# Head 0, the centroids and the last tokens' activations turned on TensorE; the means of v in one matmul per query block; a new written-out order

## The chip, the cores and the metric

One core of a Trainium2 chip runs the whole program. The metric is the device time of one execution in microseconds (us). Engine names: PE is TensorE, PEld its weight loads, DVE is VectorE, ACT is ScalarE, POOL is GpSimd, SP is SyncE, which issues most DMAs.

## The reference, cut to what matters

Three stages follow each other: attention restricted to clusters, a feed-forward layer, and a soft mixture of experts.

```python
# q, k, v: (2, 8, 768, 64); centroids: (8, 16, 64); 16 pairs of batch and head in all
q_assign = argmax(q_n @ c_n.T); k_assign = argmax(k_n @ c_n.T)
scores = where(q_assign[:, None] == k_assign[None], q @ k.T / 8, -1e9)
attn = exp(scores - max(scores)); attn /= sum(attn) + 1e-9
x = attn @ v                                   # as (1536, 512)
h = x @ w_in                                   # (512, 2048)
x = (h * clip(h + 3, 0, 6) / 6) @ w_out        # (2048, 512)
logits = x @ phi                               # 32 slots, 4 for each of 8 experts
slots = softmax(logits, over tokens).T @ x
out = softmax(logits, over slots) @ experts(slots)   # relu(s @ w1[e]) @ w2[e]
```

A query whose cluster holds no key sees only masked scores, so the softmax is even and its output is the mean of v over all keys. The kernel adds that mean separately.

## The kernel before, in words

Work is cut into *heads* i = 0 to 15 (a batch and a head, 768 queries and keys, six tiles of 128) and *tokens* t = 0 to 11 (tiles of 128 rows of x). Numbers are held as a high and a low float16 part, so that a product of two float32 numbers is made of float16 matmuls: `high` (ACT) rounds to float16, `low` (POOL) subtracts it from the float32 number.

For each head, `cast_hi` and `cast_lo` split q and k into the tile `qk1`. A DMA transpose (L356) turns its twelve 128x128 blocks into `qk1t`. `as_mm` (L385) multiplies that with the turned, normalised centroids `ct` (L793, also a DMA transpose), `as_max` finds the cluster of each row as a one-hot tile `oh` with five short DVE operations (L390 to L404), `as_put` (L411, L412) writes it next to q and k in the tile `qk2`, and a second DMA transpose (L415) gives `qk2t`. `maxq` and `maxr` (L452 on PE, L468 on DVE) take the largest masked score of each query, `shift` (L475, L477) writes it into `qk2t`, `scores` (L490, L494), `exps` (L531, L538) and `pv` (L564 to L585) make the attention output, and `finish` divides. `cnt_mm` counts the keys of each cluster and makes the mean of v for empty clusters (`mv`, a high and a low part side by side), and the last call of `pv` for a head adds it with two matmuls for each of six query blocks (L584, L585).

The input weights of the feed-forward layer are read as 64-bit numbers and narrowed to 32 bits: `narrow` is one ACT operation (L809) and three on DVE (L811, L814, L819) for each chunk of 128x1024. Chunks are called `wi` and `wod`. `wphi1` to `wphi3` fold phi into w_out.

For each token, `xtrans` turns x, `hid` (L633) multiplies with w_in, twelve matmuls of 512 columns for each of four column blocks. `act` makes the activation in halves of two column blocks: ACT (L650), DVE (L652), `high` on ACT, `low` on POOL (L322), giving `ghl`. Then each half is turned into `gt`: for tokens 0 to 5 both halves by a DMA transpose (L661); for tokens 6 to 10 the first half by a DMA transpose and the second by sixteen PE transposes into PSUM (L669) which ACT (L675) and DVE (L673) copy out; for token 11 all on PE. `logits` (L684, L685) needs both halves, then `colmax` (its transpose is L712), `dweights`, `dispatch` (L755) and `cweights`.

The end multiplies the slots with the experts' weights, 36 chunks of 1 MB called `wk`, loaded by SP. The first 15 chunks fit into buffers that are free once attention has ended; the next four take the place of w_in (`wq`), so the last of them waits for the last `hid`; the following ones wait for buffers of the last tokens' activations, and the rest for earlier chunks to be used.

The order of all this on every engine is written out by hand: each step is a generator, and `ORDER` is a list of generator numbers, each entry advancing one of them to its next `yield`. Every engine works through its own instructions in that order. `ROOMS` fixes which buffer each tile gets; PSUM has three large rooms (of `pss`) and two small ones (`psm`). SP and ACT issue DMAs in that same order, so a transfer that must wait holds back all behind it in its queue.

Of the kernel before, what the change touches and what calls it, by code (L numbers as in the profile page):

```python
# [1367 lines left out]
```

## Time and profile before

| what | value |
|---|---|
| median of three runs | 501.41 us (500.82 to 502.27) |
| the profiled execution | 496.43 us, its span 494.6 us |
| busy: PE, PEld | 439.8 us (89%), 276.1 us (56%) |
| busy: DVE, ACT, POOL | 305.0 us (62%), 310.9 us (63%), 258.1 us (52%) |
| chain that ended last, by engine | PE 61%, DVE 19%, ACT 5%, issue 4%, DMA 4%, POOL 3%, SP's queue 2% |
| moved by DMA | 96.89 MB, mean 196 GB/s |

The span runs from the first to the last instruction. The busy time of an engine is the time in which one of its instructions is on record; matmuls overlap, so a busy PE is not PE at its peak. The shares are means over stages with different limits.

### The profile page before, as it was taken

What the parts mean: (1) busy time and instruction counts of PE and PEld (TensorE: products, weight loads), DVE (VectorE), ACT (ScalarE), POOL (GpSimd) and SP (SyncE); (2) the same over time, 40 slices, a digit from 0 to 9 for tenths busy, and PEclk for the clock granted to TensorE, in tenths of its full rate; (3) what the DMA queues carried; (4) which work ended last, traced back from release to release, by engine and by line L of the source; (5) the groups of instructions that cost most, each with busy time, mean ns of one, the idle gap of its engine ahead of it and who ended that gap; (6) DMA issues with size and microseconds to landing.
All of it is one profiled execution on the core that took longest, in us unless ns stands there. A gap on an engine that the chain in (4) does not pass through costs nothing.

```text
span 494.6 us, 11908 instructions
## 1 busy us (share of the span) xinstructions
PE 439.8 (89%) x4920; PEld 276.1 (56%) x4920; DVE 305.0 (62%) x514; ACT 310.9 (63%) x551; POOL 258.1 (52%) x232
## 2 busy tenths in 40 slices
PE   0379999999999799999999999999999999678884
PEld 0236778767778565756656556664455545442343
DVE  2788988999978999859785556324243333521213
ACT  5587776798777788888857767754245445511112
POOL 4545356456966878788757858763333323400000
PEclk9999999999999999999999999999999999989998
DMA  8985963945956999917308444346998886699998
GB/s 210 257 217 129 235 176 81 194 95 156 248 125 175 245 246 196 261 40 148 88 17 166 130 118 89 126 121 107 287 329 184 252 256 177 226 371 380 378 321 278
DMA packets 139447, 96.89 MB, mean 196 GB/s; under 512 B 102016, under 2 KB 125056, under 8 KB 139392
## 3 DMA queue, kind: packets, MB, share of 16 engines
q1 hardware_dynamic: 134272, 90.29, 69.0%
q10 hardware_dynamic: 5120, 5.83, 3.5%
q8 instruction: 38, 0.62, 0.5%
q14 instruction: 17, 0.14, 0.1%
HBM read 64.06 MB, written 7.34 MB: 144 GB/s over the span
## 4 chain that ended last, share of the span: by engine, by line
PE 61%; DVE 19%; ACT 5%; issue 4%; DMA 4%; POOL 3%; SPq 2%; DVEq 0%; ACTq 0%; POOLq 0%
PE h L633 21%; DVE m L468 6%; PE st L490 5%; PE st L494 5%; PE acc L564 4%; PE sm L452 4%; PE e L1237 3%; PE acc L577 2%; PE acc L569 2%; PE acc L570 2%; POOL ghl L322 2%; SPq L947 1%; PE o L1274 1%; DVE r L652 1%; DMA qf<-in_q_dram 1%
## 5 line engine op out<-in xcount | busy, mean ns | idle before, releaser
L322 POOL TENSOR_TENSOR pp<-p,pp 128x768 f16<-128x768 f32 x64 | 115.3, 1807 | 43.1 <-ACT pp L315 30.6
L633 PE MATMUL h<-wq,xt 128*128 128x512 f16 x576 | 133.9, 379 | 0.0
L468 DVE TENSOR_REDUCE m<-sm 128x1 f32<-128x768 f32 x96 | 89.5, 952 | 21.7 <-PE sm L452 20.9
L633 PEld LDWEIGHTS <-xt 128*128 128x128 f16 x576 | 53.4, 98 | 60.7 <-issue 4.2
L322 POOL TENSOR_TENSOR ghl<-r,ghl 128x1024 f16<-128x1024 f32 (+1 forms) x25 | 50.3, 2011 | 65.4 <-ACT ghl L315 60.1
L538 ACT ACTIVATE p<-st 128x768 f32<-128x768 f32 x64 | 51.5, 805 | 26.3 <-PE st L494 20.1
L315 ACT ACTIVATE pp<-p 128x768 f16<-128x768 f32 x64 | 53.8, 841 | 5.0 <-PE acc L577 3.8
L652 DVE SCALAR_TENSOR_TENSOR r<-r,h 128x1024 f32<-128x1024 f32 (+1 forms) x26 | 29.6, 1138 | 36.1 <-ACT r L650 36.0
L452 PE MATMUL sm<-qk2t 80*128 80x384 f16 x192 | 48.3, 343 | 3.5 <-DVE m L468 3.2
L490 PE MATMUL st<-qk1t 128*128 128x384 f16 x192 | 48.6, 336 | 2.3 <-DVE m L468 1.9
L494 PE MATMUL st<-qk2t 102*128 102x384 f16 x192 | 48.6, 335 | 0.7 <-DVE qk2t L477 0.7
L564 PEld LDWEIGHTS acc<-v,pp 128*128 128x128 f32 x384 | 46.0, 192 | 2.9 <-PE st L494 0.7
L564 PE MATMUL acc<-v,pp 128*128 128x65 f32 x384 | 47.1, 274 | 0.3 <-DVE xa L597 0.3
L650 ACT ACTIVATE r<-h,b_relu 128x1024 f32<-128x1024 f32 (+1 forms) x26 | 27.2, 1046 | 15.6 <-PE h L633 9.4
L322 POOL TENSOR_TENSOR qk<-qf,qk 128x384 f16<-128x384 f32 x16 | 15.4, 962 | 39.5 <-ACT qk L315 36.9
L315 ACT ACTIVATE ghl<-r 128x1024 f16<-128x1024 f32 (+1 forms) x26 | 25.6, 988 | 15.4 <-DVE r L652 11.1
L569 PE MATMUL acc<-v,pp 128*128 128x65 f16 x384 | 32.2, 192 | 0.9 <-DVE mv L437 0.9
L531 ACT ACTIVATE pp<-st 128x768 f32<-128x768 f32 x32 | 25.4, 803 | 11.4 <-PE st L494 11.3
L570 PE MATMUL acc<-v,pp 128*128 128x64 f16 x384 | 32.2, 194 | 0.0
L385 PE MATMUL as<-ct,qk1t 128*128 128x16 f16 x384 | 12.1, 170 | 21.0 <-DMA ct<-cin 12.8
L569 PEld LDWEIGHTS <-pp 128*128 128x128 f16 x384 | 27.7, 99 | 5.3 <-issue 1.9
L570 PEld LDWEIGHTS <-pp 128*128 128x128 f16 x384 | 26.0, 96 | 4.1 <-issue 1.1
(185 smaller groups left out, 804.0 us busy)
## 6 DMA issues: line engine op xcount, KB each, us to landing
wk<-in_moe_w_dram SPq DMA_DIRECT2D x60, 512.0 KB, 7.2
wi<-in_moe_w_in_dram SPq DMA_DIRECT2D x16, 512.0 KB, 5.3
wod<-in_moe_w_out_dram SPq DMA_DIRECT2D x16, 512.0 KB, 5.7
wos<-wo ACTq DMA_DIRECT2D x8, 512.0 KB, 4.4
wk<-wos SPq DMA_DIRECT2D x8, 512.0 KB, 4.4
qf<-in_q_dram SPq DMA_DIRECT2D x16, 192.0 KB, 3.0
kf<-in_k_dram SPq DMA_DIRECT2D x16, 192.0 KB, 3.2
vf<-in_v_dram SPq DMA_DIRECT2D x16, 192.0 KB, 3.0
```

What stands on the lines that cost most here:

```text
L315: nc.scalar.activation(out, in_, AF.Copy, scale=scale)
L322: (nc.vector if e == "v" else nc.gpsimd).tensor_tensor(out=out, in0=in_, in1=hi, op=ALU.subtract)
L452: nc.tensor.matmul(s[:, j, 0:384], d["qk2t"][0:80, n], d["qk2t"][0:80, NT + 3 * j : NT + 3 * j + 3], start=True, stop=True,)
L468: nc.vector.tensor_reduce(out=d["m"][:, n : n + 1], in_=s[:, :, 0:384], op=ALU.max, axis=AX.XY)
L490: nc.tensor.matmul(s[:, j, 0:384], d["qk1t"][:, NT + t], d["qk1t"][:, 3 * j : 3 * j + 3], start=True, stop=False)
L494: nc.tensor.matmul(s[:, j, 0:384], d["qk2t"][0 : 96 + NT, NT + t], d["qk2t"][0 : 96 + NT, 3 * j : 3 * j + 3], start=False, stop=True,)
L538: nc.scalar.activation(p32, s[:, :, 0:384], AF.Exp, scale=sc_exp)
L564: nc.tensor.matmul(o, p32[:, j, r * P : (r + 1) * P], d["v32"][:, t], start=(t == 0 and n == 0), stop=False)
L569: nc.tensor.matmul(o, hi, v1[:, t, 0:65], start=(t == 0 and n == 0), stop=False)
L570: nc.tensor.matmul(o[:, 0:64], hi, v1[:, t, 65:129], start=False, stop=False)
L633: nc.tensor.matmul(s[:, fb % 2], xt[:, lhs], wq[fb][:, hl, kk], start=(n == 0), stop=(n == 11))
L652: nc.vector.scalar_tensor_tensor(out=g, in0=r, scalar=6.0 * SG, in1=sf, op0=ALU.min, op1=ALU.mult)
```

## The change

It has six parts.

1. Head 0's `qk1` and `qk2` are turned by twelve PE transposes each, into a large PSUM room, copied out by ACT (first half) and DVE (second half), instead of two DMA transposes. Heads 1 to 15 keep theirs.
2. The centroids are turned by two PE transposes and a DVE copy.
3. The first halves of tokens 8, 9 and 10 are turned on PE like their second halves.
4. `mv` holds its high part on partitions 64 to 79 and its low part on 80 to 95. `as_put` writes the one-hot twice (32 columns), so one matmul for each query block adds both.
5. In `wphi3`, two DVE operations become one on ACT and one on POOL.
6. `ORDER` and `ROOMS` are new throughout.

```diff
+    def turned(i, nm, out, t):
+        if i:
+            nc.sync.dma_start_transpose(out=out, in_=t.rearrange("p a n d -> p (a n d)"))
+            return
+        tp = pss(f"t0_{nm}").bitcast(F16)
+        for a in range(2):
+            for n in range(NT):
+                nc.tensor.transpose(tp[:, a, n * P : (n + 1) * P], t[:, a, n], ident16)
+        yield
+        for a, fn in ((0, nc.scalar.copy), (1, nc.vector.tensor_copy)):
+            fn(out[:, a * NT : (a + 1) * NT], tp[:, a, 0 : NT * P].rearrange("p (n q) -> p n q", q=P))
...
-        nc.sync.dma_start_transpose(out=d["qk1t"], in_=t.rearrange("p a n d -> p (a n d)"))
+        yield from turned(i, "qk1", d["qk1t"], t)
...
-        nc.sync.dma_start_transpose(out=d["qk2t"], in_=z.rearrange("p a n d -> p (a n d)"))
+        yield from turned(i, "qk2", d["qk2t"], z)
...
-                nc.tensor.matmul(o, e, mv[64:96, 0:65], start=False, stop=False)
-                nc.tensor.matmul(o[:, 0:64], e, mv[64:96, 65:129], start=False, stop=(n == NT - 1))
+                nc.tensor.matmul(o, e, mv[64:96], start=False, stop=(n == NT - 1))
...
-        if t < NT or (f0 == 0 and t < NTOK - 1):
+        if t < NT or (f0 == 0 and t < NTOK - 4):
             nc.sync.dma_start_transpose(
...
-        nc.sync.dma_start_transpose(out=ct, in_=cin.rearrange("p a d -> p (a d)"))
+        tp = psm("ctt").bitcast(F16)
+        for a in range(2):
+            nc.tensor.transpose(tp[:, a * P : (a + 1) * P], cin[:, 2 * a : 2 * a + 2].rearrange("p a d -> p (a d)"), ident16)
+        yield
+        nc.vector.tensor_copy(ct, tp[:, 0 : 2 * P].rearrange("p (a q) -> p a q", q=P))
...
-        nc.vector.tensor_copy(wp2[:, 4 * j : 4 * j + 4, 0:NS], wf)
-        nc.vector.tensor_tensor(
-            out=wp2[:, 4 * j : 4 * j + 4, NS : 2 * NS], in0=wf, in1=wp2[:, 4 * j : 4 * j + 4, 0:NS], op=ALU.subtract
-        )
+        high("a", wp2[:, 4 * j : 4 * j + 4, 0:NS], wf)
+        yield
+        low("p", wp2[:, 4 * j : 4 * j + 4, NS : 2 * NS], wf, wp2[:, 4 * j : 4 * j + 4, 0:NS])
...
 ORDER = (
-    "3 0 3 0 6 1 6 3 6 6 787 4 7 54 4 7 7 3 101 2 8 7 54 788 54 788 789 55 8 101 54 793 55 11 150 11 12 9 2 9 790 10 "
+    "3 3 0 2 6 0 6 6 1 7 11 11 12 4 4 6 7 7 2 787 3 7 54 7 3 54 788 3 101 54 54 788 8 103 793 55 101 789 790 8 55 "
```

What the new order does is seen in the engines' instructions. First, DVE at the start of the program, before the change; `nw` is the narrowing of a chunk of w_in, `as`, `mx` and `oh` are head 0's cluster assignment.

```order
L791 COPY cin_139<-cin_139 128x64
L811 TENSOR_SCALAR nw_i0_0_219<-nw_i0_0_219 128x1024
L814 SCALAR_TENSOR_TENSOR nw_i0_0_219<-wi_0_0_146,nw_i0_0_219 128x1024
L390 TENSOR_REDUCE mx_0_225<-as_0_191 128x12
L391 TENSOR_TENSOR as_0_191<-as_0_191,mx_0_225 128x192
L399 TENSOR_TENSOR as_0_191<-as_0_191,rank_87 128x192
L402 TENSOR_REDUCE mx2_0_252<-as_0_191 128x12
L404 TENSOR_TENSOR oh_0_254<-as_0_191,mx2_0_252 128x192
L819 SCALAR_TENSOR_TENSOR wi_0_0_146<-wi_0_0_146,nw_i0_0_219 128x1024
```

The same place after the change:

```order
L814 COPY cin_209<-cin_209 128x64
L350 COPY qk1t_0_172<-t0_qk1_173 128x768
L820 COPY ct_92<-ctt_220 128x256
L838 TENSOR_SCALAR nw_i0_0_224<-nw_i0_0_224 128x1024
L841 SCALAR_TENSOR_TENSOR nw_i0_0_224<-wi_0_0_198,nw_i0_0_224 128x1024
L846 SCALAR_TENSOR_TENSOR wi_0_0_198<-wi_0_0_198,nw_i0_0_224 128x1024
L406 TENSOR_REDUCE mx_0_267<-as_0_232 128x12
L407 TENSOR_TENSOR as_0_232<-as_0_232,mx_0_267 128x192
L415 TENSOR_TENSOR as_0_232<-as_0_232,rank_88 128x192
L418 TENSOR_REDUCE mx2_0_278<-as_0_232 128x12
L420 TENSOR_TENSOR oh_0_280<-as_0_232,mx2_0_278 128x192
```

Two copies out of PSUM have come in, and all three narrowing operations of the first chunk now stand ahead of head 0's assignment, where only two did.

Second, ACT after the change, where `as_put` of head 0 (L428, L434) stands behind the first step of the second chunk's narrowing (L836 of `nw_i0_1`); before, that chunk's step came after `as_put`.

```order
L836 ACTIVATE nw_i0_0_224<-wi_0_0_198 128x1024
L318 ACTIVATE qk1_1_216<-qf_1_166 128x6x64
L318 ACTIVATE qk1_1_216<-kf_1_168 128x6x64
L318 ACTIVATE qf_2_227<-qf_2_227 128x384
L836 ACTIVATE nw_i0_1_271<-wi_0_1_259 128x1024
L374 COPY qk2_1_103<-qk1_1_216 128x6x64
L375 COPY qk2_1_103<-qk1_1_216 128x6x64
L428 ACTIVATE qk2_0_102<-oh_0_280 128x6x32
L434 ACTIVATE qk2_0_102<-oh_0_280 128x6x32
```

`as_put` thus has one load more from HBM ahead of it in its queue than it had.

Third, DVE near the end of the tokens, before the change; `r` is an activation in float32, `gt` the copy of a turned half, `l4` and `lt` belong to the logits; the first number in a name is the token.

```order
L652 SCALAR_TENSOR_TENSOR r_10_0_6160<-r_10_0_6160,h_10_0_6094 128x1024
L703 TENSOR_REDUCE cx_8_6164<-l_all_92 128x1
L764 SCALAR_TENSOR_TENSOR zacc_93<-zacc_93,al_8_6087,z_8_6132 128x512
L673 COPY gt_9_6129<-gp_9_2_6187 128x1024
L703 TENSOR_REDUCE cx_3_6220<-l_all_92 128x1
L652 SCALAR_TENSOR_TENSOR r_10_1_6222<-r_10_1_6222,h_10_1_6168 128x1024
L691 TENSOR_TENSOR l4_9_6263<-la_9_6261,lg_9_6224 128x128
```

The same place after the change:

```order
L675 SCALAR_TENSOR_TENSOR r_10_0_6096<-r_10_0_6096,h_10_0_6039 128x1024
L787 SCALAR_TENSOR_TENSOR zacc_94<-zacc_94,al_8_6072,z_8_6100 128x512
L696 COPY gt_9_6113<-gp_9_0_6114 128x1024
L696 COPY gt_9_6113<-gp_9_2_6160 128x1024
L675 SCALAR_TENSOR_TENSOR r_10_1_6155<-r_10_1_6155,h_10_1_6076 128x1024
L714 TENSOR_TENSOR l4_9_6215<-la_9_6213,lg_9_6179 128x128
```

Both halves of token 9 are copied ahead of token 10's second activation; on PE the transposes of the second half (`gp_9_2`) have moved from before to behind the last `hid` of token 10, directly ahead of token 9's logits.

## Rows read from the trace of the kernel before

**Rows 1.** Stages: stretch and length; busy of PE, PEld, DVE, ACT, POOL (instructions); PEclk, DMA share, GB/s.

```profile
40.00:160.00 120.00, 115.22 (x1340) 90.49 (x1339) 109.22 (x160) 93.40 (x163) 72.89 (x55) 1.00 0.65 161
...
200.00:340.00 140.00, 137.99 (x1697) 85.98 (x1694) 84.14 (x143) 102.99 (x161) 98.80 (x64) 1.00 0.47 116
340.00:412.00 72.00, 71.24 (x559) 35.64 (x557) 24.06 (x53) 33.31 (x63) 25.24 (x24) 1.00 0.88 238
...
425.20:484.80 59.60, 47.24 (x552) 22.43 (x553) 16.99 (x43) 12.64 (x39) 3.96 (x14) 0.97 1.00 348
```

**Rows 2.** Timeline of the first 25 us: start, length, engine, instruction [idle before, releaser].

```profile
5.65 0.91 POOL L322 TENSOR_TENSOR qk<-qf,qk 128x384 f16<-128x384 f32 x1 [5.21 <-ACT qk L315]
...
7.64 0.18 DVE L791 COPY cin<-cin 128x64 f16<-128x64 f16 x1
...
11.63 0.90 SPq L828 DMA_DIRECT2D wi<-in_moe_w_in_dram  x2
...
12.08 1.10 ACT L809 ACTIVATE nw_i<-wi 128x1024 f32<-128x1024 f32 x1
...
12.78 0.79 PE L385 MATMUL as<-ct,qk1t 128*128 128x16 f16 x24 [12.78 <-DMA ct<-cin]
...
13.21 0.69 DVE L811 TENSOR_SCALAR nw_i<-nw_i 128x1024 uint32<-128x1024 uint32 x1 [5.39 <-ACT nw_i L809]
...
13.94 1.82 DVE L814 SCALAR_TENSOR_TENSOR nw_i<-wi,nw_i 128x1024 uint32<-128x1024 uint32 x1
...
15.68 0.34 DVE L390 TENSOR_REDUCE mx<-as 128x12 f32<-128x192 f32 x1
...
17.60 1.22 DVE L819 SCALAR_TENSOR_TENSOR wi<-wi,nw_i 128x1024 uint32<-128x1024 uint32 x1
...
18.55 1.57 SPq L415 DMA_TRANSPOSE qk2t<-qk  x1
...
22.46 2.10 PE L452 MATMUL sm<-qk2t 80*128 80x384 f16 x6
```

**Rows 3.** Tokens' end: two PE rows, then SP's waits (total, times, longest), then SP.

```profile
417.95 1.05 PE L669 MATMUL gp<-ident,ghl 128*128 128x128 f16 x16 [0.92 <-DVE r L652]
...
422.44 2.75 PE L633 MATMUL h<-wq,xt 128*128 128x512 f16 x12
...
SPq L966 <- PE h L633: 8.9, 2, 7.5
...
425.23 0.33 SPq L966 DMA_DIRECT2D wk<-in_moe_w_dram  x1
```

**Rows 4.** Weight loads of head 0's first maxima, one for each matmul of 384 columns.

```profile
22.75 0.15 PEld L452 LDWEIGHTS <-qk2t 80*128 80x128 f16 x1 [0.17 <-issue]
23.07 0.15 PEld L452 LDWEIGHTS <-qk2t 80*128 80x128 f16 x1 [0.17 <-issue]
```

**Rows 5.** Weight loads of head 0's matmuls that add the mean of v.

```profile
58.04 0.10 PEld L584 LDWEIGHTS <-qk2t 32*128 32x128 f16 x1
58.08 0.09 PEld L585 LDWEIGHTS <-qk2t 32*128 32x128 f16 x1
58.10 0.09 PEld L584 LDWEIGHTS <-qk2t 32*128 32x128 f16 x1
```

**Rows 6.** Groups by line and shape: xcount | busy us, mean ns of one | idle before, releasers.

```profile
L669 PE MATMUL gp<-ident,ghl 128*128 128x128 f16 x112 | 7.9, 219 | 1.4 <-DVE r L652 0.9 <-POOL ghl L322 0.4
L675 ACT COPY gt<-gp 128x1024 f16<-128x1024 f16 x7 | 7.1, 1011 | 4.5 <-PE gp L669 3.8 <-DMA wk<-in_moe_w_dram 0.7
L585 PE MATMUL acc<-mv,qk2t 32*128 32x64 f16 x96 | 8.0, 189 | 0.0
L905 DVE TENSOR_TENSOR wp<-wpf,wp 128x128 f16<-128x128 f32 x4 | 5.5, 1381 | 0.1
L673 DVE COPY gt<-gp 128x1024 f16<-128x1024 f16 x7 | 4.8, 689 | 6.1 <-ACT gt L675 5.6 <-PE gp L669 0.5
L904 DVE CAST wp<-wpf 128x128 f16<-128x128 f32 x4 | 3.3, 823 | 0.4 <-ACT wpf L902 0.4
```

More of the change, by code (lines that the diff above doesn't have):

```diff
@@ L271, in clustered_attention_ffn_softmoe @@
     ones = cp.tile([P, 1], F16, name="ones")
-    wmean = cp.tile([P, C], F16, name="wmean")
+    wmean = cp.tile([P, 2 * C], F16, name="wmean")
+    second = cp.tile([P, 1], F32, name="second")
     rank = cp.tile([P, C], F32, name="rank")
@@ L285, in clustered_attention_ffn_softmoe @@
     qk2 = [ap.tile([P, 2, NT, P], F16, name=f"qk2_{i}", bufs=1) for i in range(NZ)]
-    v1s = [ap.tile([P, NT, 129], F16, name=f"v1_{i}", bufs=1) for i in range(NV)]
+    v1s = [ap.tile([P, NT, 130], F16, name=f"v1_{i}", bufs=1) for i in range(NV)]
     v32s = [ap.tile([P, NT, 65], F32, name=f"v32_{i}", bufs=1) for i in range(3)]
-    mvs = [ap.tile([P, 129], F16, name=f"mv_{i}", bufs=1) for i in range(3)]
+    mvs = [ap.tile([P, 65], F16, name=f"mv_{i}", bufs=1) for i in range(3)]
     def consts():
@@ L297, in consts @@
         for t in qk2:
-            nc.gpsimd.memset(t[:, :, :, 80:128], 0.0)
+            nc.gpsimd.memset(t[:, :, :, 96:128], 0.0)
             nc.gpsimd.memset(t[:, 1, :, 96 : 96 + NT], SH)
@@ L302, in consts @@
             nc.gpsimd.memset(t[:, :, 64:65], 1.0)
+        for t in v1s:
+            nc.gpsimd.memset(t[:, :, 129:130], 0.0)
         nc.gpsimd.memset(ones, 1.0)
-        for t in mvs:
-            nc.gpsimd.memset(t[64:96], 0.0)
+        nc.vector.tensor_reduce(out=second[64:96], in_=ident[64:96, 80:96], op=ALU.max, axis=AX.X)
         nc.gpsimd.memset(b_relu, 3.0 * SG)
@@ L410, in as_put @@
         oh = d["oh"]
-        nc.scalar.activation(z[:, 0, :, 64:80], oh[:, 0:NT], AF.Copy, scale=MASK)
-        nc.scalar.activation(z[:, 1, :, 64:80], oh[:, NT:], AF.Copy, scale=MASK, bias=-MASK)
+        nc.scalar.activation(
+            z[:, 0, :, 64:96].rearrange("p n (r c) -> p n r c", r=2),
+            oh[:, 0:NT].unsqueeze(2).to_broadcast([P, NT, 2, C]),
+            AF.Copy,
+            scale=MASK,
+        )
+        nc.scalar.activation(
+            z[:, 1, :, 64:96].rearrange("p n (r c) -> p n r c", r=2),
+            oh[:, NT:].unsqueeze(2).to_broadcast([P, NT, 2, C]),
+            AF.Copy,
+            scale=MASK / 2,
+            bias=-MASK / 2,
+        )
         yield
         d["qk2t"] = ap.tile([P, 2 * NT, P], F16, tag="qk2t", name=f"qk2t_{i}", bufs=4)
-        nc.sync.dma_start_transpose(out=d["qk2t"], in_=z.rearrange("p a n d -> p (a n d)"))
+        yield from turned(i, "qk2", d["qk2t"], z)
     def cnt_mm(i):
         d = st[i]
-        oh = d["oh"]
+        z = qk2[i % NZ]
         v1 = v1s[i % NV]
@@ L423, in cnt_mm @@
         for n in range(NT):
-            nc.tensor.matmul(pm[64:80, 400:401], oh[:, NT + n], ones, start=(n == 0), stop=(n == NT - 1))
+            nc.tensor.matmul(pm[64:96, 400:401], z[:, 1, n, 64:96], ones, start=(n == 0), stop=(n == NT - 1))
         for n in range(NT):
-            nc.tensor.matmul(pm[64:80, 0:65], wmean, v1[:, n, 0:65], start=(n == 0), stop=False)
-            nc.tensor.matmul(pm[64:80, 0:64], wmean, v1[:, n, 65:129], start=False, stop=(n == NT - 1))
+            nc.tensor.matmul(pm[64:96, 0:65], wmean, v1[:, n, 0:65], start=(n == 0), stop=False)
+            nc.tensor.matmul(pm[64:96, 0:65], wmean, v1[:, n, 65:130], start=False, stop=(n == NT - 1))
         yield
         emp = sm.tile([P, 1], F32, tag="emp", name=f"emp_{i}", bufs=2)
-        nc.vector.tensor_scalar(out=emp[64:80], in0=pm[64:80, 400:401], scalar1=0.5, scalar2=None, op0=ALU.is_lt)
+        nc.vector.tensor_scalar(out=emp[64:96], in0=pm[64:96, 400:401], scalar1=(0.5 - S) * MASK / 2, scalar2=None, op0=ALU.is_lt)
         yield
@@ L434, in cnt_mm @@
         nc.vector.tensor_scalar(
-            out=mv[64:80, 0:65], in0=pm[64:80, 0:65], scalar1=emp[64:80], scalar2=None, op0=ALU.mult
+            out=mv[64:96], in0=pm[64:96, 0:65], scalar1=emp[64:96], scalar2=second[64:96], op0=ALU.mult, op1=ALU.mult
         )
         nc.vector.scalar_tensor_tensor(
-            out=mv[64:80, 65:129],
-            in0=pm[64:80, 0:64],
-            scalar=emp[64:80],
-            in1=mv[64:80, 0:64],
-            op0=ALU.mult,
-            op1=ALU.subtract,
+            out=mv[64:96], in0=pm[64:96, 0:65], scalar=emp[64:96], in1=mv[64:96], op0=ALU.mult, op1=ALU.subtract
         )
@@ L453, in maxq @@
                 s[:, j, 0:384],
-                d["qk2t"][0:80, n],
-                d["qk2t"][0:80, NT + 3 * j : NT + 3 * j + 3],
+                d["qk2t"][0:96, n],
+                d["qk2t"][0:96, NT + 3 * j : NT + 3 * j + 3],
                 start=True,
@@ L569, in pv @@
             nc.tensor.matmul(o, hi, v1[:, t, 0:65], start=(t == 0 and n == 0), stop=False)
-            nc.tensor.matmul(o[:, 0:64], hi, v1[:, t, 65:129], start=False, stop=False)
+            nc.tensor.matmul(o, hi, v1[:, t, 65:130], start=False, stop=False)
         yield
```

325 rows, old and new, of tables (ORDER, ROOMS) are left out of this document.

## The prediction

> **What bounds the kernel now.** I read the busy time of each engine by stage first, then the timelines of the two ends, then the groups of the instructions that the change touches.
>
> By stage [rows 1]: from 40 to 160 us PE is on record for 115.22 of 120 us and DVE for 109.22, so both are nearly full and one's saving passes only if the other lets it. From 200 to 340 us PE has 137.99 of 140 and DVE 84.14: PE alone leads. From 340 to 412 us PE has 71.24 of 72. From 425.2 to 484.8 us the DMA share is 1.00 and PE has 47.24 of 59.6: the experts' weights stream as fast as they come. A saving before 425 us moves the whole stream, a saving behind it is worth nothing.
>
> The start [rows 2] is a chain that PE waits in. The low part of q is made from 5.65 us, head 0's first products start at 12.78, released by the transfer that turns the centroids (PE had been idle until then), the cluster assignment runs on DVE from 15.68 to 17.60, a second transposing transfer is issued at 18.55, and the first maxima start at 22.46.
>
> The tokens' end [rows 3]: the last `hid` matmuls start at 422.44 and take 2.75, and the weights that take w_in's place are issued by SP at 425.23, after 8.9 us of such waiting. From there to the end of the span are 494.6 - 425.2 = 69.4 us of streaming. Both orders have the same pieces behind that point, so I keep the 69.4 and ask only when the last `hid` ends.
>
> **The change, part by part.** The profiled execution took 496.43 us, 1.0% under the median of 501.41; the sum below is made against 496.43 and its difference is then put on the median.
>
> *Start (parts 1, 2, 6).* The products for the assignment no longer wait for two transfers. Three low parts of 0.91 from 5.65 [rows 2] end near 8.4. Six PE transposes of one half follow the last of them. Matmuls of 384 columns come 0.32 apart this early [rows 4]; a block of 128 columns is a third, 0.107, so six take 0.64: 9.1. The copy of a half (768 columns) out of PSUM is 0.75 of a copy of 1024, which takes 0.689 on DVE and 1.011 on ACT [rows 6]: 0.52 and 0.76. So 9.6, and with a short copy of the turned centroids (an estimate of 0.2; `cin` is done at 7.82 [rows 2]) 9.8. The products then run 0.79 to about 10.6 instead of 13.57: 2.9 us earlier.
>
> Not all of that arrives. All three narrowing operations of the first chunk now stand ahead of the assignment on DVE, 0.69 + 1.82 + 1.22 = 3.7 us, and they start when ACT's step ends. That step begins at 12.08 and takes 1.10 now; it has fewer operations ahead, so I let it begin between 10.0 and 12.08, and the narrowing ends between 14.8 and 16.9. The five assignment operations, 1.92 together, then end between 16.7 and 18.8, against 17.60 now. Behind them come the wider `as_put` (estimate 0.7), twelve blocks (1.3) and an eviction (0.76) in place of a transfer: together 2.8 against the 4.9 from 17.60 to 22.46. The first maxima start between 19.5 and 21.6, at best 18.9 if the steps overlap: a gain of 0.9 to 3.6. I take **-2.3**. The end of no gain stays, because `as_put` is queued on ACT behind the second chunk's step, whose load was issued at 11.63 [rows 2]; if it lands late, `as_put` waits, and with it everything of head 0.
>
> *Means of v (part 4).* There are 96 matmuls fewer [rows 6]. Weight loads of the pair follow each other at 58.04, 58.08 and 58.10 us [rows 5], about 0.06 for a pair, so one is worth 0.031: 96 x 0.031 = 3.0 us at most, and 0 at the other end. The mean of 189 ns [rows 6] is a pipelined length and says nothing about the pace. In heads 8 to 15 PE leads, so their half (1.5) counts in full; in heads 0 to 7 DVE is nearly as full, so I count half of theirs: **-2.2**. Products of 96 rows instead of 80, and of 65 columns instead of 64, I cost at nothing: a `hid` matmul of 128 rows goes at 2.75 / 12 / 512 = 0.45 ns a column [rows 3], those of 32 rows at 0.031 / 64 = 0.48, so rows are free, and 36 matmuls with v's low part in each of 16 heads get one column more, 576 x 0.5 ns = 0.3 us, inside the rounding.
>
> The Trainium skill ("Perfetto Trace Analysis", section "Identifying the Most-Contended Engine") holds that the matmul row is a poor measure of how close PE is to its limit, since matmuls are pipelined, and that weight-load busy time is a better one. In this trace PEld has 85.98 of 140 us where PE has 137.99 [rows 1]; by that rule PE would have room and the term of the means would be 0 instead of -2.2.
>
> *Turned first halves of tokens 8 to 10 (part 3).* 48 more transposes on PE. Sixteen took 1.05 us [rows 3], so halves of tokens 8 and 9, which fall where PE leads, cost 0.9 to 1.05 each, about 1.8 to 2.1. Token 10's falls where PE waits anyway, but the chain gets longer: DVE has both copies of token 9 ahead of token 10's second activation, and the logits of token 9 stand directly behind the transposes of its second half on PE, so they wait for the copies, 1.011 on ACT or 0.689 on DVE [rows 6]. Part of that is hidden by `hid` of token 11. I take **+2.4**, with +1.8 as the lower bound (transposes alone) and +8 as the upper (below, first slower rival). In return SP loses three transposing transfers; SP's queue waits for `hid` there anyway [rows 3], so that is 0.
>
> *The fold of phi (part 5).* DVE loses 3.3 + 5.5 = 8.8 us [rows 6], which ACT and POOL take up. Where this runs, PE leads and all three have idle time [rows 1]: **0**. Cover gone would mean DVE in the way in the stretch up to 160; I bound the gain at -2.
>
> *New order elsewhere:* 0, as no row of before can price it. It is the largest unknown; the bounds of the other terms stand in for it.
>
> Sum: -2.3 - 2.2 + 2.4 + 0 + 0 = **-2.1 us**: 494.3 against 496.43, and 501.41 - 2.1 = **499.3 us** for the median.
>
> **Rivals.** About 0.3%, 1.5 us, is what a measurement of this kernel can tell from no change.
>
> *Forecast as above*, 497.3 to 501.3 (each gain a little more or less): 0.42, of which about a quarter falls within 0.3% (above 499.9).
>
> *The gains don't pass.* PE has room where the 96 matmuls went (0), while start and tail come as forecast: -2.3 + 0 + 2.4 = +0.1, **501.5 us**. The same comes out if the start is held by the narrowing and the second chunk's load (0) and only the means' gain pays for the tail: -2.2 + 2.4 = +0.2. For it: two queues in which `as_put` stands behind more than before, and DVE's 109.22 of 120 us [rows 1]. Against it: PE's 137.99 of 140. Chance 0.18. The skill's rule on weight loads, named above, points this way.
>
> *Slower: the turned halves hold the tail.* In the new order the large PSUM rooms go from `h` of a token to a turned half and back to `h`; a room comes free only when both its copies are done. If each of the three tokens waits for its transposes (about 1.0) and both copies (1.011 + 0.689 [rows 6]) in a row, it costs 2.7 x 3 = 8.1 instead of 2.4: -2.3 - 2.2 + 8.1 = +3.6, **505.0 us**. It decides against the kernel from about 2 us for a token, since 3 x 2 - 4.5 = +1.5. For it: the row of transposes there waited 0.92 for DVE already [rows 3], and ACT's copies waited 3.8 of 4.5 us on PE's transposes [rows 6]. Against it: three rooms, and 12 `hid` matmuls of 2.75 us between. Chance 0.18.
>
> *Larger gain.* Start -3.6, means -3.0, tail +1.8, DVE's relief -2: -6.8, **494.6 us**. For it: DVE and PE are both near full up to 160 us, and this change takes work from both. Chance 0.20.
>
> *The transposes don't overlap.* 48 at their recorded mean of 0.219 [rows 6] are 10.5, where sixteen in 0.96 give 2.9 (the middle of 0.9 to 1.05, three times): 501.41 - 2.1 + 7.6 = **506.9 us**. Sixteen in 1.05 us [rows 3] speaks against it: 0.02. The Trainium skill ("TensorE: Matmul & The Clock Gate", Part 4 "PE-mode transpose") states about 275 ns for a transpose in a kernel's context; by that figure, which I call an estimate, 48 would take 13.2 us and the sum would be +8.2, but the sixteen in 1.05 us of this trace stand against it.
>
> **The numbers.** Range 494.0 to 504.5: it takes in the forecast, the case of no gain, most of the larger gain and of the slow tail; outside are the far half of the slow tail, the last rival and gains beyond 7 us. Faster by over 0.3%: three quarters of 0.42 and the 0.20, about 0.52. Slower: 0.18 + 0.02 and a little of the case of no gain, 0.21. The same: the rest of the case of no gain and a quarter of 0.42, 0.27.
>
> **What the profile after would show.** Start: the first maxima begin at 19 to 21.6 us; if at 22.4 or later, the narrowing or the second load holds them, and DVE's row of the first assignment operation names ACT or a DMA. Means: L608 96 times and no second line; PE's busy time from 200 to 340 falls by less than its idle time grows if the term is 0. Tail: the last `hid` ends at about 423.1 (425.2 - 2.1) and SP issues the next weights there; if logits wait for copies over 1 us a token, the slow tail is there. End: some 69 us from that point to the end of the span; if not, the stream depends on something I left out. The prediction is wrong if the new order opens or closes waits in the middle of the kernel by more than 2 us, which no row of before can show.

## The result and the profile after

The kernel after takes 492.72 us (median of 20, 489.84 to 498.30), the kernel before 500.68 (median of 20, 496.95 to 507.49). The ratio is **0.9848, 95% interval 0.9818 to 0.9879**: 1.5% faster, about 7.6 us, where 2.1 were forecast. The ratios leave out executions more than 1.5% above the fastest of their kernel; ranges and groups of times below count all, since what parts them bears on the cause.

The profiled execution of after took 489.88 us, its span 488.1 against 494.6. By stage, in the columns of [rows 1]:

```profile
40.00:160.00 120.00, 117.48 (x1365) 92.51 (x1362) 113.37 (x170) 99.84 (x168) 81.56 (x57) 1.00 0.69 170
...
200.00:340.00 140.00, 138.75 (x1608) 84.55 (x1605) 76.67 (x135) 102.60 (x164) 99.69 (x65) 1.00 0.51 110
340.00:403.00 63.00, 61.49 (x536) 32.04 (x535) 23.59 (x50) 30.70 (x58) 19.34 (x10) 1.00 0.77 247
416.20:477.40 61.20, 50.56 (x556) 23.95 (x559) 17.09 (x44) 13.64 (x43) 5.50 (x26) 0.90 1.02 343
```

PE is fuller from 40 to 160 us by 2.3 us, and DVE by 4.2; the streaming at the end goes at 343 GB/s where it went at 348. The start, to be held against [rows 2], in the timeline:

```profile
9.16 0.82 PE L347 MATMUL t_qk<-ident,qk 128*128 128x128 f16 x6 [1.57 <-POOL qk L325]
...
10.02 0.80 ACT L350 COPY qk1t<-t_qk 128x768 f16<-128x768 f16 x1 [2.33 <-PE t_qk L347]
...
12.38 1.10 ACT L836 ACTIVATE nw_i<-wi 128x1024 f32<-128x1024 f32 x1
...
13.51 0.69 DVE L838 TENSOR_SCALAR nw_i<-nw_i 128x1024 uint32<-128x1024 uint32 x1 [1.91 <-ACT nw_i L836]
...
16.09 1.81 DVE L846 SCALAR_TENSOR_TENSOR wi<-wi,nw_i 128x1024 uint32<-128x1024 uint32 x1
...
17.83 0.34 DVE L406 TENSOR_REDUCE mx<-as 128x12 f32<-128x192 f32 x1
...
20.28 1.46 PE L347 MATMUL t_qk<-ident,qk 128*128 128x128 f16 x12 [7.83 <-ACT qk L428]
...
22.61 0.56 DVE L350 COPY qk2t<-t_qk 128x768 f16<-128x768 f16 x1 [0.93 <-ACT qk2t L350]
...
23.22 1.12 PE L476 MATMUL sm<-qk2t 96*128 96x384 f16 x3 [0.85 <-DVE qk2t L350]
```

The narrowing still stands ahead of the assignment, and the first maxima start 0.76 us later than before, not 2.3 earlier. The 0.76 belongs to this pair: over the five profiles below in which the old order turns head 0 by transfers, the first maxima start between 22.46 and 24.53 us, over the four of the new order that turn it on PE and keep that start, between 22.69 and 23.22. The tokens' end, which answers to [rows 3], in PE's and SP's rows of the timeline:

```profile
400.92 0.20 PE L707 MATMUL lg<-wp,gt 128*128 128x64 f16 x1 [0.85 <-ACT gt L698]
...
401.88 2.75 PE L656 MATMUL h<-wq,xt 128*128 128x512 f16 x12
...
407.51 1.07 PE L692 MATMUL gp<-ident,ghl 128*128 128x128 f16 x16
...
411.44 0.20 PE L707 MATMUL lg<-wp,gt 128*128 128x64 f16 x1 [0.66 <-ACT gt L698]
...
413.48 2.75 PE L656 MATMUL h<-wq,xt 128*128 128x512 f16 x12
...
416.26 1.75 SPq L992 DMA_DIRECT2D wk<-in_moe_w_dram  x4
```

The last `hid` ends 9.0 us earlier (416.2 against 425.2). The groups that answer to [rows 6]:

```profile
L608 PE MATMUL acc<-mv,qk2t 32*128 32x65 f16 x96 | 5.6, 190 | 0.1
...
L325 POOL TENSOR_TENSOR wp<-wpf,wp 128x128 f16<-128x128 f32 x4 | 1.7, 431 | 1.8 <-ACT wp L318 1.8
L318 ACT ACTIVATE wp<-wpf 128x128 f16<-128x128 f32 x4 | 1.2, 312 | 0.0
```

The fold of phi costs 2.9 us on ACT and POOL together, where DVE had spent 8.8.

**Three stretches.** To place gains, I cut each profiled execution at two marks of the timeline: the start of DVE's 41st maximum (the expectations call it the fortieth) and the end of the last `hid`. But for falls of the clock, the middle stretch repeats within 0.3 us in runs that share its program, so it tells small differences that the times do not.

| us | order | start | middle | end | span | ratio to before |
|---|---|---|---|---|---|---|
| before | old | 114.3 | 310.9 | 69.4 | 494.6 | 1 |
| before_again | old | 114.8 | 316.2 | 71.8 | 502.9 | |
| after | new | 113.2 | 303.0 | 71.8 | 488.1 | 0.9848 |
| old_ops_new_order | new | 121.3 | 308.1 | 71.4 | 500.8 | 1.0006 |
| two_mean_matmuls | new | 114.2 | 304.3 | 71.7 | 490.2 | 0.9895 |
| fold_on_dve | new | 113.9 | 307.3 | 72.0 | 493.2 | 0.9907 |
| dma_first_halves | new | 119.6 | 303.1 | 71.8 | 494.5 | 0.9820 |
| dma_head0 | new | 119.9 | 303.1 | 71.9 | 494.9 | 0.9939 |
| one_mean_old_order | old | 114.7 | 310.5 | 75.5 | 500.8 | 1.0008 |
| fold_old_order | old | 113.8 | 316.7 | 73.0 | 503.4 | 1.0021 |
| head0_old_order | old | 118.0 | 311.0 | 74.0 | 503.1 | 1.0111 |
| before_filler | old | 113.1 | 311.8 | 69.5 | 494.4 | 0.9983 |

Between the two profiled executions the start gives 1.1 us, the middle 7.9, and the end takes 2.4 back. The middle of before, of after and of old_ops_new_order, in the columns of [rows 1]:

```profile
114.30:425.20 310.90, 300.61 (x3319) 186.40 (x3317) 193.34 (x321) 213.78 (x358) 194.42 (x132) 1.00 0.67 170
```

```profile
113.20:416.20 303.00, 297.33 (x3258) 184.57 (x3256) 187.31 (x312) 215.32 (x359) 190.26 (x124) 1.00 0.64 165
```

```profile
121.30:429.40 308.10, 299.69 (x3282) 184.94 (x3278) 190.22 (x317) 210.44 (x352) 189.30 (x120) 0.99 0.68 168
```

PE's idle time there falls from 10.3 us to 5.7, its busy time from 300.6 to 297.3.

### The profile page after: what moved, and what is told of

Same layout as the page of the kernel before. It is cut to its first block, busy times and chain, and to the rows that moved or that the text cites. A ratio compares the mean times of both kernels' runs of the same rounds, so it can differ in the third digit from the quotient of the medians.

```text
span 488.1 us, 11871 instructions
## 1 busy us (share of the span) xinstructions
PE 442.7 (91%) x4898; PEld 279.7 (57%) x4898; DVE 304.0 (62%) x513; ACT 319.6 (65%) x560; POOL 260.2 (53%) x236
## 4 chain that ended last, share of the span: by engine, by line
PE 70%; DVE 17%; ACT 5%; issue 3%; DMA 2%; SPq 1%; POOL 1%; ACTq 0%; DVEq 0%
PE h L656 25%; PE acc L588 6%; DVE m L492 5%; PE st L514 5%; PE st L518 4%; PE sm L476 4%; PE e L1263 3%; PE acc L601 2%; PE acc L593 2%; PE acc L594 2%; PE o L1300 2%; PE gp L692 2%; PE z L778 2%; DVE nw_i L841 2%; DVE wi L846 1%
## 5 line engine op out<-in xcount | busy, mean ns | idle before, releaser
L325 POOL TENSOR_TENSOR pp<-p,pp 128x768 f16<-128x768 f32 x64 | 113.1, 1769 | 55.3 <-ACT pp L318 26.7
L325 POOL TENSOR_TENSOR ghl<-r,ghl 128x1024 f16<-128x1024 f32 (+1 forms) x25 | 51.3, 2052 | 65.2 <-ACT ghl L318 65.1
L476 PE MATMUL sm<-qk2t 96*128 96x384 f16 x192 | 47.5, 341 | 3.7 <-DVE m L492 1.8
L514 PE MATMUL st<-qk1t 128*128 128x384 f16 x192 | 47.6, 329 | 1.8 <-DVE m L492 1.5
L593 PE MATMUL acc<-v,pp 128*128 128x65 f16 x384 | 32.3, 192 | 0.0
L594 PE MATMUL acc<-v,pp 128*128 128x65 f16 x384 | 32.3, 195 | 0.0
L325 POOL TENSOR_TENSOR qk<-qf,qk 128x384 f16<-128x384 f32 x16 | 17.4, 1089 | 22.9 <-ACT qk L318 21.2
L518 PEld LDWEIGHTS <-qk2t 102*128 102x128 f16 x192 | 19.0, 99 | 13.0 <-issue 0.7
```

The lines of the kernel that those rows point to most:

```text
L325: (nc.vector if e == "v" else nc.gpsimd).tensor_tensor(out=out, in0=in_, in1=hi, op=ALU.subtract)
L476: nc.tensor.matmul(s[:, j, 0:384], d["qk2t"][0:96, n], d["qk2t"][0:96, NT + 3 * j : NT + 3 * j + 3], start=True, stop=True,)
L514: nc.tensor.matmul(s[:, j, 0:384], d["qk1t"][:, NT + t], d["qk1t"][:, 3 * j : 3 * j + 3], start=True, stop=False)
L518: nc.tensor.matmul(s[:, j, 0:384], d["qk2t"][0 : 96 + NT, NT + t], d["qk2t"][0 : 96 + NT, 3 * j : 3 * j + 3], start=False, stop=True,)
L593: nc.tensor.matmul(o, hi, v1[:, t, 0:65], start=(t == 0 and n == 0), stop=False)
L594: nc.tensor.matmul(o, hi, v1[:, t, 65:130], start=False, stop=False)
```

## The experiments

**The order alone.** The operations of before under the new `ORDER` and `ROOMS`.

```diff
 ORDER = (
-    "3 0 3 0 6 1 6 3 6 6 787 4 7 54 4 7 7 3 101 2 8 7 54 788 54 788 789 55 8 101 54 793 55 11 150 11 12 9 2 9 790 10 "
+    "3 3 0 2 6 0 6 6 1 7 11 11 12 4 4 6 7 7 2 787 3 7 54 7 3 54 788 3 101 54 54 788 8 103 793 55 101 789 790 8 55 "
...
-            nc.tensor.matmul(pm[64:80, 400:401], oh[:, NT + n], ones, start=(n == 0), stop=(n == NT - 1))
+            nc.tensor.matmul(pm[64:80, 400:401], z[:, 1, n, 64:80], ones, start=(n == 0), stop=(n == NT - 1))
```

> The operations of before in the new order: head 0, the centroids and the first halves of tokens 8 to 10 by transposing transfers, two matmuls for each mean of v, the fold of phi on DVE; the keys are counted from the masked one-hot in qk2, as after does, because the old buffer is reused too early in this order. Theory A, the order itself closes PE's waits between 20 and 340 us: the last projection of the last head still comes some 9 us earlier than before (12.3 in the trace of after, less 3.0 for the means), and the run is 1.0 to 2.0% faster than before. Theory B, the new operations take work from DVE, PE and the transfers and the order only follows: the waits come back, and the run is within 1% of before or slower.

Ratio 1.0006 (0.9969 to 1.0042): theory B. The order by itself makes the middle 2.8 us shorter (308.1 against 310.9), 1.9 of it idle time of PE (10.3 to 8.4), and its profiled execution loses 7.0 at the start.

**The parts, undone one by one in the new order.** First the means.

```diff
-                nc.tensor.matmul(o, e, mv[64:96], start=False, stop=(n == NT - 1))
+                nc.tensor.matmul(o, e, mv[64:96, 0:65], start=False, stop=False)
+                nc.tensor.matmul(o[:, 0:64], e, mv[64:96, 65:129], start=False, stop=(n == NT - 1))
```

> The kernel after with part 4 undone: the one-hot once, mv with both parts side by side, two matmuls for each query block. If PE is the bound where they stand, 96 x 0.031 = 3.0 us slower than after (0.6%), and the last hid ends at about 419.2 instead of 416.2. If PE has room, as the share of weight loads would have it, the same as after within 1 us.

Ratio 0.9895 (0.9858 to 0.9933), 0.5% above after's, about 2.4 us, but the two intervals overlap. The traces tell more. The last `hid` ends at 418.5, 2.3 later than in after. Of this, 0.4 was there before the first of these matmuls: the 13th maximum starts at 46.17 us against 45.73, after a fall of the clock that after doesn't have:

```profile
37.60:41.00 3.40, 3.40 (x48) 2.27 (x45) 2.76 (x6) 1.56 (x4) 1.84 (x2) 0.50 0.66 182
```

Another 0.5 comes up to the 41st maximum and 1.3 behind it, in steps of 0.16 to 0.19 at many heads: 1.8 us, where a PE that is the bound everywhere would lose 3.0. The Trainium skill ("Perfetto Trace Analysis", section "Identifying the Most-Contended Engine"), which would have given 0, does not hold here, with PEld busy for 84.55 of 140 us.

The turned first halves:

```diff
-        if t < NT or (f0 == 0 and t < NTOK - 4):
+        if t < NT or (f0 == 0 and t < NTOK - 1):
```

> The kernel after with the first halves of tokens 8, 9 and 10 turned by transfers again. Theory A, the turned halves cost PE and the waits for their copies some 3.3 us in the tail (12.3 us ahead at 340, 9.0 at the last hid): the last hid ends at about 413 and the run is 2 to 3.5 us faster than after. Theory B, the transfers hold SP's queue and the logits wait for them: the same as after, or slower by 1 to 5 us.

Ratio 0.9820 (0.9783 to 0.9857), not apart from after's, and the middle is the same to 0.1 us. Two things cancel in it. Where the transposes stood, this run's `hid` matmuls gain 0.6, 0.9 and 0.7 us on those of after, 2.2 in all, and between the second and the third they lose 2.25. Its rows there, to be held against 400.92 and 401.88 of after above:

```profile
406.43 0.20 PE L707 MATMUL lg<-wp,gt 128*128 128x64 f16 x1 [1.41 <-ACT gt L698]
...
407.39 4.44 PE L656 MATMUL h<-wq,xt 128*128 128x512 f16 x12
```

```profile
407.70:411.10 3.40, 3.40 (x10) 1.22 (x9) 0.82 (x3) 1.12 (x2) 1.70 (x1) 0.50 0.86 176
```

PE waits 1.41 us for the copies instead of 0.85, and then the clock falls under twelve `hid` matmuls: 4.44 us instead of 2.75. So the turned halves cost 2.2 us, as theory A has it in part, and in this execution the transfers cost as much; whether the clock falls there in the other five is not known.

This run showed something else. Its program is that of after up to token 8, and yet its 41st maximum comes 6.4 us later. In the stretches of its trace (columns as in [rows 1]; the third below is of after):

```profile
36.30:52.80 16.50, 16.50 (x110) 11.31 (x110) 9.43 (x16) 8.98 (x15) 8.37 (x6) 1.00 0.31 66
52.90:70.00 17.10, 17.08 (x197) 13.94 (x192) 15.44 (x25) 13.66 (x23) 5.92 (x5) 1.00 0.43 94
```

```profile
35.60:60.00 24.40, 23.57 (x265) 18.04 (x265) 23.03 (x38) 20.00 (x34) 11.40 (x9) 1.00 0.46 108
```

PE is busy all but without a gap in the first two, but does 110 matmuls in 16.5 us and then 197 in 17.1: matmuls of 384 columns come 0.32 us apart (1.2 GHz) until 52.86, and 0.16 (2.4 GHz) behind it. In after that step came at 35.57, in before at 40.59. The clock column reads 1.00 all the same: in these traces it shows the falls that come after a first rise, and not the pace before that.

Head 0 and the centroids by transfers:

```diff
+        nc.sync.dma_start_transpose(out=out, in_=t.rearrange("p a n d -> p (a n d)"))
+        yield
+        return
...
-        nc.vector.tensor_copy(ct, tp[:, 0 : 2 * P].rearrange("p (a q) -> p a q", q=P))
+        nc.sync.dma_start_transpose(out=ct, in_=cin.rearrange("p a d -> p (a d)"))
+        yield
```

> The kernel after with head 0 and the centroids turned by transfers again. As the prediction had it: 2.3 us slower than after. As the trace of after reads (first maxima at 23.22 us, 0.76 later than before, with all three narrowing operations ahead of the assignment): 0 to 2 us slower, the first maxima at 23 to 25 us, since the assignment still waits for the narrowing and only the second turn gets longer.

Ratio 0.9939 (0.9913 to 0.9965): 4.5 us slower than after, more than either reading. Its PE rows at the start:

```profile
16.50 0.79 PE L404 MATMUL as<-ct,qk1t 128*128 128x16 f16 x24 [16.50 <-DMA ct<-cin]
24.34 0.81 PE L404 MATMUL as<-ct,qk1t 128*128 128x16 f16 x24 [7.05 <-DMA qk1t<-qk]
28.02 1.46 PE L479 MATMUL sm<-qk2t 96*128 96x384 f16 x4 [2.88 <-DMA qk2t<-qk]
```

In the new order the transfers would bring the first maxima at 28.0 us. The turn on PE is worth 4.8 us there, but against this order, not against the kernel before. The 41st maximum comes 6.7 us later than in after: the other 1.9 arise between the 7th and the 13th, where this trace comes to 2.4 GHz only at 46.3 us.

The fold of phi:

```diff
-        high("a", wp2[:, 4 * j : 4 * j + 4, 0:NS], wf)
-        yield
-        low("p", wp2[:, 4 * j : 4 * j + 4, NS : 2 * NS], wf, wp2[:, 4 * j : 4 * j + 4, 0:NS])
+        nc.vector.tensor_copy(wp2[:, 4 * j : 4 * j + 4, 0:NS], wf)
+        nc.vector.tensor_tensor(
+            out=wp2[:, 4 * j : 4 * j + 4, NS : 2 * NS], in0=wf, in1=wp2[:, 4 * j : 4 * j + 4, 0:NS], op=ALU.subtract
+        )
```

> The kernel after with the two operations of the fold of phi back on DVE (part 5 undone). By the prediction 0, since PE leads there. By the traces so far, in which the stretch from the fortieth of DVE's maxima to the last hid takes 303.0 us in after and in all its twins, 304.3 with two matmuls for each mean, and 308.1 with all old operations in the new order: some 3 to 4 us in that stretch, because DVE then waits for ACT's step and its maxima come late, and 0.5 to 0.8% slower than after.

Ratio 0.9907 (0.9870 to 0.9945), 0.6% or 3.0 us above after's, and 4.3 us in the middle. The timeline shows how, and the stretch that follows what it set off:

```profile
247.13 0.28 ACT L929 ACTIVATE wpf<-wpo 128x128 f32<-128x128 f32 x1
...
247.44 0.23 DVE L931 CAST wp<-wpf 128x128 f16<-128x128 f32 x1 [1.14 <-ACT wpf L929]
...
247.90 1.82 DVE L492 TENSOR_REDUCE m<-sm 128x1 f32<-128x768 f32 x2
248.91 0.48 PE L514 MATMUL st<-qk1t 128*128 128x384 f16 x2 [1.49 <-DVE m L492]
```

```profile
249.50:252.90 3.40, 3.40 (x42) 2.26 (x40) 1.74 (x4) 2.15 (x4) 0.69 (x1) 0.50 0.08 30
```

DVE waits 1.14 us for ACT's step, its two maxima behind that come late, and PE waits 1.49 us for them. Right behind, the clock is granted at 0.50 (1.2 GHz) from 249.5 to 252.9 us, which costs another 1.5 against the same rows of after. At another fold PE waits 0.53 us for DVE at 197.5. In after DVE has none of these operations, and PE runs without a gap of 0.05 from 163.7 to 225.0 us and from 226.2 to 270. In old_ops_new_order, which has the fold on DVE too, PE has the same two waits (0.54 and 1.50) and such a fall behind the second.

**Parts put alone into the old order.**

```diff
+                nc.tensor.matmul(o, e, mv[64:96], start=False, stop=(n == NT - 1))
...
+        high("a", wp2[:, 4 * j : 4 * j + 4, 0:NS], wf)
+        low("p", wp2[:, 4 * j : 4 * j + 4, NS : 2 * NS], wf, wp2[:, 4 * j : 4 * j + 4, 0:NS])
...
+        turned(i, "qk1", d["qk1t"], t)
```

> The kernel before, its order kept, with one matmul for each query block's mean (part 4 alone). By the prediction 2.2 us faster than before (0.4%), by the difference measured in the new order (0.47 of a per cent between the kernel after and its twin with two matmuls) the same; by the rule on weight loads nothing.

> The kernel before, its order kept, with the fold of phi on ACT and POOL (part 5 alone). If DVE's waits for the fold cost in the old order as in the new, that stretch takes 307 to 309 us instead of 310.9, and the kernel is 0.4 to 0.7% faster than before. If the old order has other waits there, 310 to 311 and no change. The end, from the last hid to the end of the span, is 74 to 75.5 us, as in the two other runs of the old order, if the 69.4 of the profiled execution of before was that execution's own.

> The kernel before, its order kept, with head 0 and the centroids turned on PE (parts 1 and 2 alone; the copies directly behind the transposes, the constants one place earlier). By the prediction's working: the assignment still waits for two narrowing operations (13.2 to 15.7 us), as_put as before, then 1.3 + 0.8 in place of the transfer: first maxima at 20 to 20.5 us instead of 22.46, and 2 us faster than before. If the 0.9% that the turn of head 0 gives in the new order belongs to that order alone (there the transfers bring the first maxima to 28.0 us), within 1 us of before.

None gains by the times: 1.0008 (0.9971 to 1.0046), 1.0021 (0.9978 to 1.0064) and 1.0111 (1.0071 to 1.0150), the last 1.1% slower. One matmul for the means leaves the middle at 310.5 against 310.9, but with a fall of the clock that the trace of before doesn't have, behind a wait of 1.79 us at 167.1:

```profile
167.40:170.80 3.40, 3.40 (x30) 2.90 (x28) 3.04 (x5) 1.41 (x3) 2.79 (x2) 0.50 1.21 56
```

Over it the run loses 0.8 us: its 59th maximum starts 0.1 later than in before, its 61st 0.9. The rest of the middle gains 1.2, in steps of 0.16 to 0.19 at single heads as in the new order. The times can't tell that (0.2%) from nothing. Head 0 turned on PE has its first maxima at 24.55 us: the second turn stands on PE behind head 1's products, which wait for a transfer until 20.96. That alone is not its loss, for before_again has them at 24.50; but DVE's first maximum starts at 28.18 here and at 26.00 there, behind a narrowing operation that waits for ACT until 25.78. The middle of 316.7 with the fold holds a fall of the clock, the subject of the next runs; behind that fall the run gains nothing on before.

**The kernel before once more, and its wait at 134 us.**

> The kernel before once more, for its stages. If the end of its profiled execution (69.4 us from the last hid) was that execution's own, here it is 73 to 75.5 us as in the three other runs of the old order, with the stretch from the fortieth maximum to the last hid at 310 to 311 us again; if it belongs to the kernel, 69 to 70.

The end took 71.8 us. Over the six profiles in the old order it lies between 69.4 and 75.5 (mean 72.2), over the twelve in the new between 71.4 and 73.4 (mean 72.2): the means are equal, and 69.4 was that execution's own. New was the middle, 316.2. A row of its timeline, then two stretches:

```profile
135.50 0.38 PE L475 MATMUL sm<-nident,m 128*6 128x128 f32 x2 [0.91 <-DVE m L468]
```

```profile
126.50:134.50 8.00, 8.00 (x96) 6.25 (x96) 7.78 (x8) 6.23 (x12) 8.00 (x4) 1.00 1.09 257
...
138.10:148.90 10.80, 10.80 (x65) 9.29 (x64) 6.48 (x9) 6.16 (x11) 6.07 (x5) 0.55 0.55 125
```

PE waits 0.91 us for a maximum that DVE makes late, behind narrowing operations of 2.85 and 2.40 us; then the granted clock falls: 0.55 over the last stretch, 0.50 from 137.7 to 147.9 us. PE's rows come 0.52 us later than in before ahead of it and 5.18 behind it: 4.7 of the 5.3 us. The profiled execution of before had the same wait without the fall. None of the twelve profiles in the new order falls between 130 and 160 us. To see whether the wait matters:

```diff
+        for _f in range(18 if (i, n) == (8, 1) else 0):
+            nc.tensor.matmul(s[:, _f % 2, 384:512], ident16, ident16, start=True, stop=True)
```

> The kernel before with 18 matmuls of 128 columns that nothing reads, on PE behind the first maximum of head 8 and ahead of head 7's shift, where PE waits 0.91 us for DVE at 134 us in every execution of the old order, and where the granted clock fell to 0.55 from 138.1 to 148.9 us in one execution of before and one twin, for 5.4 to 5.7 us, and not in the profiled one. Theory C, that wait is what the fall hangs on: no fall between 135 and 150 us, the stretch from the fortieth maximum to the last hid at 310 to 311 us, no times above 503.5 (26 of 100 executions of before lie above 503), and the median 1 to 2 us under that of before. Theory D, the fall comes by chance whatever PE waits for: times above 503.5 as before and the same median.

The same stretch, with PE kept busy by matmuls that nothing reads:

```profile
138.10:148.90 10.80, 10.68 (x106) 8.77 (x105) 8.41 (x9) 9.43 (x17) 8.25 (x6) 1.00 0.71 174
```

106 matmuls instead of 65. All 12 executions lie between 496.24 and 501.80 us (median 500.13); of the 17 of before beside them, 9 lie above 503.5 (median 503.62). Its trace has another fall instead (0.50 from 166.6 to 170.0 us, 0.9 us of loss), so the middle is not shorter; but the late group is gone: theory C, as far as twelve executions show it.

**The start.** Two kinds of change: the assignment ahead of the narrowing, and fillers where PE waits.

```diff
-    "3 3 0 2 6 0 6 6 1 7 11 11 12 4 4 6 7 7 2 787 3 7 54 7 3 54 788 3 101 54 54 788 8 103 793 55 101 789 790 8 55 "
+    "3 3 0 2 6 0 6 6 1 7 11 11 12 4 4 6 7 7 2 787 3 7 54 7 3 54 788 3 101 54 54 8 103 793 55 101 8 55 9 9 10 10 788 "
...
+        for _f in range(FILL.get((i, n), 0)):
+            nc.tensor.matmul(s[:, _f % 2, 384:512], ident16, ident16, start=True, stop=True)
```

> The kernel after with the entries of the start in another order: head 0's assignment and as_put ahead of the three narrowing operations of the first chunk on DVE, and the second chunk's step on ACT behind as_put; the second assignment's products behind the first two maxima. The first maxima then start at about 18 to 19.5 us instead of 23.2. If the start passes on to the end, as the prediction's first term had it, 2 to 4 us faster than after; if DVE's maxima and narrowing are the bound until 40 us, the narrowing only moves behind the maxima and the time is that of after within 1.5 us.

> The kernel after with 23 matmuls of 512 columns added on PE that nothing reads (left operand the identity, right operand head 0's turned q and k): 20 between head 0's assignment products (they end at 12.45 us) and its second turn (20.28), 3 ahead of its first maxima. The work of the kernel is unchanged. Theory C, the time depends on when PE comes to its full pace (a matmul of 384 columns each 0.16 us instead of 0.32: from 35.57 us in the trace of after, from 52.86 in the run with the first halves by transfer, whose program is the same up to there): with PE busy from 12 us on, the first maxima already go at 0.16, the times above 495 us disappear, and the median is 3 to 6 us under that of after. Theory D, the stretch from 22 to 40 us is bound by DVE (16.27 of 17.6 us busy) and the pace there costs nothing: the same as after within 1.5 us, with times above 495 as before.

> The kernel after with matmuls that nothing reads put where PE waits at the start: 28 of 512 columns ahead of head 0's second turn, and 4 to 14 of 128 columns behind each of head 0's maxima from the second on, into columns that the maxima leave free. Theory C, the pace falls when PE waits between the maxima (it fell at 26.25 us in the run with fillers ahead of them only) and its rise is late by chance: without such waits the pace stays at 0.16 us for 384 columns from 23 us on, the fortieth maximum comes at 107 to 111 us instead of 113 to 120, and the run is 3 to 6 us faster than the median of after, without times above 495. Theory D, DVE bounds that stretch: the fortieth maximum at 113 and the time that of the better executions of after, 490 to 491.

> The start of assign_first (assignment ahead of the narrowing, first maxima at 17.8 us, but half pace until 44.5 us there) with such fillers: 9 ahead of the second turn, 6 to 40 of 128 columns behind each of head 0's maxima. Theory C: full pace from 18 us or soon after, the fortieth maximum at 105 to 110 us and the run 4 to 8 us faster than after. Theory D: the gain of the early start is lost behind DVE's narrowing as before, the fortieth maximum at 112 to 114 us and 490 to 492 us.

> As filler_between, with fillers behind the first maxima of head 1 too (12, 34 and 6 matmuls of 128 columns), where PE waited 0.6 and 1.8 us for DVE just before the pace fell at 35.99 us and stayed low until 52.56. Theory C: the pace stays at 0.16 us for 384 columns from 23 us to the end of the start, the fortieth maximum comes at 111 to 113 us, no time lies above 495, and the median is 2 to 4 us under that of after. Theory D, the late rise is not a matter of PE's waits: the pace falls again near 36 us or the fortieth maximum is at 117 to 120 us.

> The same with about a third more fillers, and some behind the fifth maximum of head 1. Theory C: as filler_to_37, the fortieth maximum at 111 to 114 us, where fillers in the way of real work would show as up to 2 us later. Theory D: as there.

| kernel | median us (runs) | ratio to before | first maxima | 2.4 GHz in the profiled execution | 41st maximum |
|---|---|---|---|---|---|
| after | 492.72 (20) | 0.9848 | 23.22 | from 35.57 | 113.2 |
| assign_first | 493.69 (6) | 0.9861 | 17.77 | from 44.50 | 117.3 |
| filler_matmuls | 495.49 (6) | 0.9890 | 22.89 | to 26.25, again from 53.34 | 120.1 |
| filler_between | 492.86 (6) | 0.9832 | 22.68 | to 35.99, again from 52.56 | 119.3 |
| assign_first_filler | 494.01 (6) | 0.9878 | 18.30 | to 33.83, then on and off to 43.94 | 116.3 |
| filler_to_37 | 493.69 (6) | 0.9867 | 22.36 | throughout | 112.7 |
| filler_more | 494.11 (6) | 0.9882 | 22.85 | throughout | 116.2 |

Before these falls PE had waited (in filler_between 1.76 us up to 35.99, then 16.5 us at a granted clock of 0.50); with the waits filled it did not fall:

```profile
22.40:36.00 13.60, 13.17 (x188) 10.47 (x188) 12.52 (x23) 8.17 (x18) 3.37 (x4) 1.00 1.06 249
36.00:52.00 16.00, 15.85 (x178) 12.22 (x176) 15.51 (x25) 13.26 (x23) 8.45 (x6) 1.00 0.63 142
```

So in these traces the clock hangs on the waits, as theory C has it; but with full clock throughout, the 41st maximum comes only 0.5 us before that of after, since DVE is busy for 12.52 of 13.60 us there: theory D, as to what can be gained. The six medians lie no lower than that of after; in filler_more the maxima wait for the fillers. Nor do the times above 495 us go, of which after has 8 in 20: filler_to_37 has 1 in 6 and filler_more 2, too few to tell, so that a late rise makes after's late group is likely but not shown. Assigning first brings the first maxima 5.4 us forward and loses all of it behind the narrowing and to a rise at 44.50 us. No version beats after.

## Why the prediction was wrong

The sign was right, the size a quarter of what was measured, and the time lay below the range.

**Start, -2.3: the mechanism failed.** ACT's step was not moved ahead of 12.08 but to 12.38, since ACT first waits 2.33 us for PE's transposes and then runs five operations; the third narrowing operation took 1.81 us, not 1.22; ACT's and DVE's copies ran one after the other. The narrowing ended at 17.9, outside my 14.8 to 16.9. Nor does a start of the first maxima pass on as the working had it: at 22.46 and 24.50 us in two executions of before, they are followed by the 41st at 114.3 and 114.8; at 17.77 in assign_first, by 117.3. The trace of after gains 1.1 us at the 41st maximum, which no run traces to these parts, and that of dma_first_halves, whose clock rises late, loses 5.3.

**Means of v, -2.2: right in kind, a little large.** 1.8 us by the traces in the new order, in steps of up to 0.19 for the six matmuls of a head, which is the 0.031 of the working. In the old order the middle gains 1.2 but for a fall of the clock. Both orders pass the saving on at some heads and not at others.

**Turned halves, +2.4: right in cost, wrong in what it was set against.** They cost 2.2 us; but the transfers, put at 0, cost 2.25 in this order, by a longer wait for the copies (1.41 us against 0.85) and a fall of the clock, so the middle is 303.0 or 303.1 us with or without them. That was one execution. The slower rival falls with this.

**Fold of phi, 0: the step that failed most.** "Where this runs, PE leads and all three have idle time" counted DVE's busy time, 8.8 us, against DVE's idle time. What counts is the place in DVE's queue: an operation that waits 1.14 us for ACT, ahead of maxima for which PE waits, costs PE 1.49 us and then its clock. Measured 3.0 us by the ratios, 4.3 by the trace, in the new order; in the old one nothing.

**New order, 0: 2.8 us in the middle, and none of it in the time by itself.** Together with the parts PE's idle time in the middle falls by 4.6 us, which is the sign that the prediction named, waits closed there by more than 2 us. The gain comes from order and operations together: the old operations in the new order make 1.0006, parts alone in the old order 1.0008 to 1.0111, both together 0.9848. I costed the two apart. All five parts in the old order were not tried.

**The base.** The sum was made against one execution of before, 496.43 us, and its difference put on the median. That execution had a short end (69.4 us where the mean is 72.2), which the working kept for both kernels, and no fall of the clock at 138 us, which the late half of the executions beside before_filler seems to have had. A change that closes such a wait gains more at the median than between two profiles.

The rival of a larger gain, 494.6 us, came nearest, and DVE's relief, its bound of -2, was in it, too small by half; that its time came so near is partly luck, for its gain at the start did not come. Transposes overlapped as [rows 3] showed: sixteen in 1.07 us.

## What to carry to other kernels

Busy time does not price an operation on an engine whose queue another engine waits for: look at what stands behind it there and who waits, at the worst place. Where work and a written-out order change together, cost them together, since each may gain nothing by itself. Compare stretches between marks of the timeline over several executions before trusting one profile as the base.
